# Gated mixer: one activation instruction per two PSUM banks, and the two halves of the hidden layer computed ahead of the spatial product

## The chip, the core and the metric

The kernel runs on one core of one Trainium2 chip. The engines of the core run side by side and wait for each other through semaphores: PE (TensorE, matrix products, with PEld for its weight loads), DVE (VectorE), ACT (ScalarE), POOL (GpSimd) and SP, which issues the DMA transfers. PE writes its products to PSUM, eight banks of 512 float32 columns on 128 partitions; DVE and ACT read them from there. The metric is the device time of one execution in microseconds (us).

## What is computed

Two residual blocks over 2048 tokens of width 448, in bfloat16. The first is a layer norm and a local attention with 16 heads, which the change doesn't touch. The second is a gated mixer with a spatial product over all tokens:

```python
def _B_ref(x, w_in, w_sp, b_sp, w_out):
    B, S, D = x.shape                    # 1, 2048, 448
    F = w_in.shape[-1]                   # 1792
    Fh = F // 2                          # 896
    z = _gelu(jnp.einsum('bsd,df->bsf', x, w_in))
    z1 = z[..., :Fh].copy()
    z2 = _layernorm(z[..., Fh:], axis=-1)
    g = jnp.einsum('ts,bsf->btf', w_sp, z2) + b_sp[None, :, None]
    return jnp.einsum('bsf,fd->bsd', z1 * g, w_out)

h  = x + _A_ref(_layernorm(x, axis=-1), A_wqkv, A_wo)
h2 = h + _B_ref(_layernorm(h, axis=-1), B_w_in, B_w_sp, B_b_sp, B_w_out)
```

`_gelu` is the tanh approximation. The halves of the hidden layer are called z1 (the gate) and z2 (normalised and mixed over the tokens).

## The kernel before

Every instruction is issued through `iss(engine, function, reads, writes)`. It records which resources the instruction reads and writes (`Res` objects, one for a bank, a tile or a block), and works out from that the semaphore waits. Each engine runs its own instructions strictly in the order in which the program issues them, so the order of the calls is the schedule.

The attention part ends with the rows of `x_tm` (16 blocks of 128 tokens) holding h. The mixer then goes through these steps:

- **Hidden input.** `ln_norm_block` (L351, DVE) normalises a block, `tm_transpose_block` (L360 on PE, L369 on DVE) transposes it by way of a PSUM bank into `xhT`. Eight blocks are normalised and transposed, then the other eight. The banks come from a counter over all eight banks, `banksB`, from which four draws for the bias `bb` have been made before.
- **z2.** For each of 16 blocks and each of the two halves of 448 columns, `z2_half_mm` (L744) makes four accumulating matmuls into one bank. A `GeluTile` then computes gelu as x times sigmoid of a cubic: ACT copies the bank to `xb` (`copy`, L708); DVE makes the cubic in three instructions (`front`, L712 to L714); ACT applies Sigmoid (`tanh`, L718); DVE multiplies and sums in one instruction (`back`, L723); ACT squares and sums (`sq`, L733). The steps of successive tiles are staggered by one tile. Three buffers `xb`, `wk`, `tb` rotate.
- **Normalisation of z2.** After all 32 halves, DVE turns the sums into mean and variance, a chain of 16 small instructions makes the reciprocal root (`rsqrt_chain`, L232 to L243), and 16 instructions (L787) normalise the blocks in place.
- **z1, spatial product, gate, output.** A tile is one of 7 chunks of 128 hidden columns (`fc`) by one of 4 chunks of 512 tokens (`tc`). For tile j the program issues the z1 matmuls (`z1_tile_mm`, L755, four of them) and their gelu; for tile j-1 the spatial product (`g_tile_mm`, L800, 16 accumulating matmuls, one for each block of z2); for tile j-2 the gate (`u_tile`, L813 and L815, DVE adds the bias and multiplies with z1 in place). After the seventh tile of a token chunk, `wout_block` makes the output product of four token blocks (L823, seven matmuls each), adds the residual on DVE (L827) and stores (L829, by SP).

The weights `wspT_lo`, `wspT_hi` and `w_out` are loaded by DMAs that SP issues early; the change does not move them.

Of the kernel before, what the change touches and what calls it, by code (L numbers as in the profile page):

```python
# [6 lines left out]
D = 448  # L7
# [22 lines left out]
GELU_C = 0.044715  # L30
GELU_K2 = 1.5957691216057308
# [96 lines left out]
def bass_sequential_preLN__sliding_local_dilated__mixer_gmlp__prompt_kernel(  # L128
# [17 lines left out]
    with contextlib.ExitStack() as top:  # L146
# [20 lines left out]
        s3a = sb("s3a", [128, 2, NB], F32)  # L167
        s3b = sb("s3b", [128, 2, NB], F32)
        junk = sb("junk", [128, 512], BF16)
        junk2 = sb("junk2", [128, 512], BF16)  # L170
# [28 lines left out]
        r_junk2 = Res("junk2")  # L199
# [435 lines left out]
        NGW = 3  # L635
        xb = sb("xb", [128, NGW, 512], BF16, es=stackB)
        wk = sb("wk", [128, NGW, 512], BF16, es=stackB)
        tb = sb("tb", [128, NGW, 512], BF16, es=stackB)
        w_out = sb("w_out", [128, FC7, D], BF16, es=stackB)
        ub = sb("ub", [128, 2, 512], BF16, es=stackB)  # L640
# [15 lines left out]
        r_z2ph = [[bres("z2p_%d_%d" % (m, k)) for k in range(2)] for m in range(NB)]  # L656
        r_s3 = []
        r_xb = [bres("xb%d" % i) for i in range(NGW)]
        r_wk = [bres("wk%d" % i) for i in range(NGW)]
        r_tb = [bres("tb%d" % i) for i in range(NGW)]  # L660
        r_wout = bres("w_out")
        r_ub = [bres("ub0"), bres("ub1")]
# [11 lines left out]
        banksB = gbanks_B  # L674
        gctr = [0]
# [9 lines left out]
        class GeluTile:  # L685
            def __init__(self, out_dst_ap, in_ps_ap, n, rdst, rbank, sum_x_ap=None, sum_sq_ap=None):
                s = gctr[0] % NGW
                gctr[0] += 1
                self.s = s
                self.XB = xb[:, s, 0:n]  # L690
                self.WK = wk[:, s, 0:n]
                self.TB = tb[:, s, 0:n]
                self.out_dst_ap = out_dst_ap
                self.in_ps_ap = in_ps_ap
                self.n = n
                self.rdst = rdst
                self.rbank = rbank
                self.sum_x_ap = sum_x_ap
                self.sum_sq_ap = sum_sq_ap
                if sum_x_ap is not None:  # L700
                    self.rsx = Res("sumx")
                    self.rsq = Res("sumsq")
                    r_s3.append(self.rsx)
                    r_s3.append(self.rsq)

            def copy(self):
                s = self.s
                iss("act", lambda e: e.activation(self.XB, self.in_ps_ap, AF.Copy), reads=[self.rbank], writes=[r_xb[s]])  # L708

            def front(self):  # L710
                s = self.s
                iss("dve", lambda e: e.tensor_tensor(self.WK, self.XB, self.XB, ALU.mult), reads=[r_xb[s]], writes=[r_wk[s]])  # L712
                iss("dve", lambda e: e.tensor_scalar(self.WK, self.WK, GELU_C, 1.0, ALU.mult, ALU.add), reads=[r_wk[s]], writes=[r_wk[s]])  # L713
                iss("dve", lambda e: e.tensor_tensor(self.WK, self.WK, self.XB, ALU.mult), reads=[r_wk[s], r_xb[s]], writes=[r_wk[s]])  # L714

            def tanh(self):
                s = self.s
                iss("act", lambda e: e.activation(self.TB, self.WK, AF.Sigmoid, scale=GELU_K2), reads=[r_wk[s]], writes=[r_tb[s]])  # L718

            def back(self):  # L720
                s = self.s
                if self.sum_x_ap is not None:
                    iss("dve", lambda e: e.tensor_tensor_reduce(self.out_dst_ap, self.TB, self.XB, 1.0, 0.0, ALU.mult, ALU.add,  # L723
                                                               self.sum_x_ap),
                        reads=[r_tb[s], r_xb[s]], writes=[self.rdst, self.rsx])
                else:
                    iss("dve", lambda e: e.tensor_tensor(self.out_dst_ap, self.TB, self.XB, ALU.mult),
                        reads=[r_tb[s], r_xb[s]], writes=[self.rdst])

            def sq(self):  # L730
                if self.sum_sq_ap is None:
                    return
                iss("act", lambda e: e.activation(junk2[:, 0:self.n], self.out_dst_ap, AF.Square, accum_out=self.sum_sq_ap),  # L733
                    reads=[self.rdst], writes=[r_junk2, self.rsq])

        def hn_unit(m):
            ln_norm_block(m, mv2, rstd2, r_ln2, m % NTR)
            tm_transpose_block(m, m % NTR, banksB, "dve")

        def z2_half_mm(m, k):  # L740
            bk = banksB.next()
            out_ap = psum[:, bk * 512: bk * 512 + D]
            for c in range(NCH):
                iss("pe", lambda e, c=c: e.matmul(out_ap, xhT[0:DC, c, PAD + 128 * m: PAD + 128 * m + 128],  # L744
                                                 w_in[:, c, FH + D * k: FH + D * (k + 1)],
                                                 start=(c == 0), stop=(c == NCH - 1)),
                    reads=[r_xhT[m], r_win], writes=[r_bank[bk]])
            return GeluTile(z2p[:, m, D * k:D * (k + 1)], out_ap, D, r_z2ph[m][k], r_bank[bk],
                            s3a[:, k, m:m + 1], s3b[:, k, m:m + 1])

        def z1_tile_mm(fc, tc):
            bk = banksB.next()
            out_ap = psum[:, bk * 512: bk * 512 + 512]
            for c in range(NCH):
                iss("pe", lambda e, c=c: e.matmul(out_ap, w_in[:, c, fc * 128:(fc + 1) * 128],  # L755
                                                 xhT[0:DC, c, PAD + 512 * tc: PAD + 512 * (tc + 1)],
                                                 start=(c == 0), stop=(c == NCH - 1)),
                    reads=[r_win] + r_xhT[4 * tc:4 * tc + 4], writes=[r_bank[bk]])
            return GeluTile(z1p[:, fc, 512 * tc:512 * (tc + 1)], out_ap, 512, r_z1p[fc][tc], r_bank[bk])

        for half in range(2):
            for m in range(8 * half, 8 * half + 8):
                ln_norm_block(m, mv2, rstd2, r_ln2, m % NTR)
            for m in range(8 * half, 8 * half + 8):
                tm_transpose_block(m, m % NTR, banksB, "dve")
        NH = 2 * NB
        live = {}
        for j in range(NH + 3):
            if j < NH:
                m, k = j // 2, j % 2  # L770
                g = z2_half_mm(m, k)
                live[j] = g
                g.copy()
                g.front()
            if 0 <= j - 1 < NH:
                live[j - 1].tanh()
                live[j - 1].back()
            if 0 <= j - 2 < NH:
                live[j - 2].sq()
                del live[j - 2]  # L780

        iss("dve", lambda e: e.tensor_tensor(s3a[:, 0, :], s3a[:, 0, :], s3a[:, 1, :], ALU.add), reads=[r_ln3] + r_s3, writes=[r_ln3])
        iss("dve", lambda e: e.tensor_tensor(s3b[:, 0, :], s3b[:, 0, :], s3b[:, 1, :], ALU.add), reads=[r_ln3], writes=[r_ln3])
        mean_var_from_sums(s3a[:, 0, :], s3b[:, 0, :], float(FH), mv3, r_ln3)
        rstd3 = rsqrt_chain(lambda: mv3[:, 0:NB, 1], 0, NB, EPS, 3, r_ln3)
        for m in range(NB):
            iss("dve", lambda e, m=m: e.tensor_scalar(z2p[:, m, :], z2p[:, m, :], mv3[:, m, 0:1], rstd3[:, m:m + 1],  # L787
                                                     ALU.subtract, ALU.mult),
                reads=[r_z2ph[m][0], r_z2ph[m][1], r_ln3], writes=[r_z2ph[m][0], r_z2ph[m][1]])
# [3 lines left out]
        def g_tile_mm(fc, tc):  # L793
            bk = banksB.next()
            out_ap = psum[:, bk * 512: bk * 512 + 512]
            wsrc = wspT_lo if tc < 2 else wspT_hi
            coff = 512 * (tc % 2)
            hhi = 0 if tc < 2 else 1
            for sbk in range(NB):
                iss("pe", lambda e, sbk=sbk: e.matmul(out_ap, z2p[:, sbk, fc * 128:(fc + 1) * 128],  # L800
                                                     wsrc[:, sbk, coff:coff + 512],
                                                     start=(sbk == 0), stop=(sbk == NB - 1)),
                    reads=[r_z2ph[sbk][0], r_z2ph[sbk][1], r_wspT[2 * sbk + hhi]], writes=[r_bank[bk]])
            gbank[(fc, tc)] = (bk, out_ap)
# [3 lines left out]
        def u_tile(fc, tc):  # L808
            bk, out_ap = gbank[(fc, tc)]
            utile = z1p[:, fc, 512 * tc:512 * (tc + 1)]  # L810
            s = uct[0] % 2
# [6 lines left out]
        def wout_block(m):  # L818
            tc = m // 4
            bk = banksB.next()  # L820
# [73 lines left out]
```

## Time and profile before

| | |
|---|---|
| median of 3 runs | 344.4 us (339.64 to 347.36) |
| span of the profiled execution | 342.4 us |
| mean granted clock of PE in it | 0.915 |
| end of the attention, start of the mixer's hidden input | about 127 us |
| first z2 matmul | 135.6 us |
| first matmul of the spatial product | 196.1 us |
| last residual addition begins | 339.7 us |

The profile is of one execution of its own. Its span runs from the first to the last instruction; the device times of the three runs stand beside it, and no separate device time is given for the profiled one. A row of the timeline is: start in us, duration in us, engine, line, operation, output<-input, shapes, count, and in brackets the idle time ahead of it and the engine that ended it. A row of a group is: line, engine, operation, names, shapes, count, then total busy us and mean ns of one, then the idle time before. A row of the stretches is: from:to, length, busy time and count of instructions (x) of PE, PEld, DVE, ACT and POOL, the granted clock of PE as a share of full speed, the DMA share and GB/s. A row of the chain is start, duration and what ran.

### The profile page before, as it was taken

The page shows a single profiled execution, that of the slowest core. Times are in us where ns is not written, and L with a number is a line of the kernel's source. Part 1 is how long each engine was busy: PE and PEld are TensorE (multiplying, and loading weights), DVE is VectorE, ACT ScalarE, POOL GpSimd, SP SyncE. Part 2 cuts the span into 40 slices and gives each one's busy share as a digit, 9 for nine tenths or more (in the row PEclk, how much of TensorE's full clock was granted, in tenths as well). Part 3 has the DMA queues.
Part 4 walks back from the last instruction along what each step waited for, and adds up shares of the span by engine and source line. Part 5 has one row for each costly group of instructions (what it writes and reads, how often), then busy time and mean ns, then how long its engine had stood idle before and what let it go on. Part 6 is the DMA issues. An engine that isn't in the chain of part 4 may idle for free.

```text
span 342.4 us, 4998 instructions
## 1 busy us (share of the span) xinstructions
PE 287.6 (84%) x1859; PEld 144.9 (42%) x1872; DVE 242.8 (71%) x670; ACT 156.8 (46%) x320; POOL 5.1 (1%) x17
## 2 busy tenths in 40 slices
PE   3789899999998848966550099999999999999996
PEld 1434455555565617521110034444444444444442
DVE  4987446897779779899999896554555565545554
ACT  1435878777866020899999322221222022212220
POOL 5000000000000000000000000000000000000000
PEclk9879989999987556999996589999999999999999
DMA  7999900000000069930000000001000100000001
GB/s 223 258 220 179 190 16 2 2 0 2 3 2 1 2 162 187 161 76 0 0 1 1 0 2 0 0 2 50 3 3 0 38 17 0 0 26 30 1 0 54
DMA packets 40537, 16.39 MB, mean 48 GB/s; under 512 B 34177, under 2 KB 39617, under 8 KB 40514
## 3 DMA queue, kind: packets, MB, share of 16 engines
q1 hardware_dynamic: 40514, 16.08, 22.5%
q8 instruction: 14, 0.23, 0.3%
q14 instruction: 9, 0.07, 0.1%
HBM read 5.85 MB, written 1.84 MB: 22 GB/s over the span
## 4 chain that ended last, share of the span: by engine, by line
PE 66%; DVE 28%; ACT 2%; issue 2%; DMA 1%; ACTq 0%; DVEq 0%
PE psum L800 29%; PE psum L383 9%; PE psum L755 7%; PE psum L823 6%; DVE z2p L723 5%; PE psum L400 4%; PE psum L485 4%; PE psum L444 4%; DVE wk L714 3%; DVE wk L712 3%; DVE wk L713 3%; DVE xhT L369 2%; DVE tring L351 2%; PE psum L416 2%; DVE st L347 1%
## 5 line engine op out<-in xcount | busy, mean ns | idle before, releaser
L708 ACT ACTIVATE xb<-psum 128x448 bf16<-128x448 f32 (+1 forms) x60 | 33.4, 558 | 108.3 <-PE psum L755 95.5
L800 PE MATMUL psum<-wspT_lo,z2p 128*128 128x512 bf16 x217 | 52.7, 388 | 17.9 <-DVE z2p L787 17.4
L712 DVE TENSOR_TENSOR wk<-xb 128x448 bf16<-128x448 bf16 (+1 forms) x60 | 24.2, 404 | 40.1 <-ACT xb L708 40.1
L800 PE MATMUL psum<-wspT_hi,z2p 128*128 128x512 bf16 x218 | 49.7, 379 | 0.3
L423 ACT ACTIVATE E<-psum 128x456 bf16<-128x456 f32 (+1 forms) x72 | 39.6, 550 | 15.1 <-PE psum L472 8.8
L800 PEld LDWEIGHTS psum<-wspT_lo,z2p 128*128 128x128 bf16 x224 | 21.9, 98 | 46.9 <-DVE z2p L787 22.3
L718 ACT ACTIVATE tb<-wk 128x448 bf16<-128x448 bf16 (+1 forms) x60 | 35.9, 598 | 12.7 <-DVE wk L714 12.7
L744 PE MATMUL psum<-w_in,xhT 112*128 112x448 bf16 x128 | 28.7, 365 | 11.1 <-ACT xb L708 11.1
L800 PEld LDWEIGHTS psum<-wspT_hi,z2p 128*128 128x128 bf16 x224 | 21.9, 98 | 26.5
L755 PE MATMUL psum<-xhT,w_in 112*128 112x512 bf16 x112 | 28.8, 379 | 1.2 <-ACT xb L708 1.2
L714 DVE TENSOR_TENSOR wk<-wk,xb 128x448 bf16<-128x448 bf16 (+1 forms) x60 | 24.5, 408 | 2.1
L744 PEld LDWEIGHTS psum<-w_in,xhT 112*128 112x128 bf16 x128 | 11.4, 101 | 28.0 <-ACT xb L708 19.0
L444 PEld LDWEIGHTS psum<-V,E 128*114 128x114 bf16 (+1 forms) x288 | 21.4, 149 | 2.4 <-issue 0.4
L823 PE MATMUL psum<-w_out,z1p 128*128 128x448 bf16 x112 | 22.0, 353 | 0.1
L444 PE MATMUL psum<-V,E 128*114 128x29 bf16 (+1 forms) x288 | 21.7, 210 | 0.0
L485 PE MATMUL psum<-wo,OT 112*128 112x448 bf16 x64 | 18.4, 420 | 3.9 <-DVE OT L475 2.8
L432 DVE TENSOR_TENSOR E<-E,maskb 128x1824 bf16<-128x1824 bf16 (+1 forms) x18 | 19.9, 1103 | 1.8 <-ACT E L423 1.7
L813 DVE TENSOR_TENSOR ub<-psum,bb 128x512 bf16<-128x512 f32 x28 | 19.1, 683 | 2.3 <-PE psum L800 2.3
L723 DVE CUSTOM_DVE_ANT_0 z2p<-tb,xb 128x448 bf16<-128x448 bf16 x32 | 19.8, 618 | 0.9 <-ACT tb L718 0.8
L383 PE MATMUL psum<-xhT,wqp 112*128 112x512 bf16 x64 | 18.1, 440 | 2.3 <-DVE xhT L369 2.3
L827 DVE TENSOR_TENSOR tring<-psum,x_tm 128x448 bf16<-128x448 f32 x16 | 10.0, 624 | 13.5 <-PE psum L823 13.5
L713 DVE TENSOR_SCALAR wk<-wk 128x448 bf16<-128x448 bf16 (+1 forms) x60 | 17.1, 285 | 2.1
(82 smaller groups left out, 338.1 us busy)
## 6 DMA issues: line engine op xcount, KB each, us to landing
x_tm<-in_A_x_dram SPq DMA_DIRECT2D x4, 448.0 KB, 7.2
out_dram<-tring SPq DMA_DIRECT2D x16, 112.0 KB, 1.7
w_in<-in_B_w_in_dram SPq DMA_DIRECT2D x1, 1568.0 KB, 15.5
stg<-in_A_wqkv_dram SPq DMA_DIRECT2D x1, 1176.0 KB, 9.9
w_out<-in_B_w_out_dram SPq DMA_DIRECT2D x1, 784.0 KB, 4.5
wo<-in_A_wo_dram SPq DMA_DIRECT2D x1, 392.0 KB, 12.9
wspT_lo<-in_B_w_sp_dram SPq DMA_TRANSPOSE x16, 4.0
wspT_hi<-in_B_w_sp_dram SPq DMA_TRANSPOSE x16, 4.1
```

The lines of the kernel that those rows point to most:

```text
L383: e.matmul(out_ap, wsrc[:, c, gg, :], xhT[0:DC, c, col0:col0 + 512], start=(c == 0), stop=(c == NCH - 1)),
L423: iss("act", lambda e, in_ap=in_ap, out_e=out_e: e.activation(out_e, in_ap, AF.Exp, scale=SCALE), reads=[r_bank[hh]], writes=[r_E[slot]])
L444: e.matmul(psum[0:nq, ob + h * 32: ob + h * 32 + DH + 1], E[0:nk, slot, eidx, 0:nq], V1[0:nk, vslot, h, 0:DH + 1]),
L708: iss("act", lambda e: e.activation(self.XB, self.in_ps_ap, AF.Copy), reads=[self.rbank], writes=[r_xb[s]])
L712: iss("dve", lambda e: e.tensor_tensor(self.WK, self.XB, self.XB, ALU.mult), reads=[r_xb[s]], writes=[r_wk[s]])
L714: iss("dve", lambda e: e.tensor_tensor(self.WK, self.WK, self.XB, ALU.mult), reads=[r_wk[s], r_xb[s]], writes=[r_wk[s]])
L718: iss("act", lambda e: e.activation(self.TB, self.WK, AF.Sigmoid, scale=GELU_K2), reads=[r_wk[s]], writes=[r_tb[s]])
L723: iss("dve", lambda e: e.tensor_tensor_reduce(self.out_dst_ap, self.TB, self.XB, 1.0, 0.0, ALU.mult, ALU.add, self.sum_x_ap), reads=[r_tb[ ...
L744: iss("pe", lambda e, c=c: e.matmul(out_ap, xhT[0:DC, c, PAD + 128 * m: PAD + 128 * m + 128], w_in[:, c, FH + D * k: FH + D * (k + 1)], st ...
L755: iss("pe", lambda e, c=c: e.matmul(out_ap, w_in[:, c, fc * 128:(fc + 1) * 128], xhT[0:DC, c, PAD + 512 * tc: PAD + 512 * (tc + 1)], start ...
L800: iss("pe", lambda e, sbk=sbk: e.matmul(out_ap, z2p[:, sbk, fc * 128:(fc + 1) * 128], wsrc[:, sbk, coff:coff + 512], start=(sbk == 0), sto ...
L823: iss("pe", lambda e, fc=fc: e.matmul(out_ap, z1p[:, fc, 128 * m:128 * m + 128], w_out[:, fc, :], start=(fc == 0), stop=(fc == FC7 - 1)), ...
```

## The change

Gelu becomes one ACT instruction (`Gelu_apprx_tanh`) that reads two neighbouring PSUM banks and writes the result; the class `GeluTile` with its buffers goes. Banks for z2 and z1 are drawn in pairs from a counter of their own, `PairBanks`, which goes round four pairs. The sums for the layer norm of z2 are made by DVE (`bn_stats` on each half of a block, `bn_aggr` on both), and z2 is normalised after every four blocks instead of after all 16. All z2 blocks come first, then all z1 pairs (128 hidden columns by 1024 tokens), then the spatial product with the gate. The output product of a token chunk is issued after the first product tile of the next chunk; for the last chunk, six of seven matmuls of each of the four blocks come ahead, then the seventh of each with the residual and the store. The bias buffer `ub` has three slots instead of two.

```diff
+        banksB = Banks([0, 1, 2, 3, 4, 5, 6, 7])
+        class PairBanks:
+            def next(self):
+                p = self.i % 4
+                self.i += 1
+                return 2 * p
...
+        def z2_block(m):
+            bk = pairs.next()
+            for k in range(2):
+                out_ap = psum[:, (bk + k) * 512: (bk + k) * 512 + D]
+                for c in range(NCH):
+                    iss("pe", ... e.matmul(out_ap, xhT[0:DC, c, PAD + 128 * m: PAD + 128 * m + 128],
+                                 w_in[:, c, FH + D * k: FH + D * (k + 1)], ...),
+                        reads=[r_xhT[m], r_win], writes=[r_bank[bk + k]])
+            src = psum[:, bk * 512: (bk + 2) * 512].rearrange("p (k n) -> p k n", k=2)[:, :, 0:D]
+            dst = z2p[:, m, :].rearrange("p (k n) -> p k n", k=2)
+            iss("act", lambda e: e.activation(dst, src, AF.Gelu_apprx_tanh),
+                reads=[r_bank[bk], r_bank[bk + 1]], writes=[r_z2p[m]])
+            for k in range(2):
+                iss("dve", lambda e, k=k: e.bn_stats(st3[:, m, k, :], z2p[:, m, D * k:D * (k + 1)]),
+                    reads=[r_z2p[m], r_st3[m]], writes=[r_st3[m]])
+            iss("dve", lambda e: e.bn_aggr(mv3[:, m, :], st3[:, m, :, :]), reads=[r_st3[m]], writes=[r_mv3[m]])
+
+        def z2_finish(lo, hi):
...
+            rstd3 = rsqrt_chain(lambda: mv3[:, lo:hi, 1], lo, hi, EPS, 3, r_ln3)
+            for m in range(lo, hi):
+                iss("dve", lambda e, m=m: e.tensor_scalar(z2p[:, m, :], z2p[:, m, :], mv3[:, m, 0:1],
+                                                         rstd3[:, m - lo:m - lo + 1],
+                                                         ALU.subtract, ALU.mult),
+                    reads=[r_z2p[m], r_ln3], writes=[r_z2p[m]])
+
+        def z1_pair(fc, th):
+            bk = pairs.next()
+            for t in range(2):
+                tc = 2 * th + t
+                out_ap = psum[:, (bk + t) * 512: (bk + t) * 512 + 512]
...
+            src = psum[:, bk * 512: (bk + 2) * 512]
+            dst = z1p[:, fc, 1024 * th:1024 * (th + 1)]
+            iss("act", lambda e: e.activation(dst, src, AF.Gelu_apprx_tanh),
+                reads=[r_bank[bk], r_bank[bk + 1]], writes=[r_z1p[fc][2 * th], r_z1p[fc][2 * th + 1]])
...
+        for m in range(NB):
+            z2_block(m)
+            if m % 4 == 3:
+                z2_finish(m - 3, m + 1)
+        for th in range(2):
+            for fc in range(FC7):
+                z1_pair(fc, th)
         tiles = [(fc, tc) for tc in range(4) for fc in range(FC7)]
+        for j, (fc, tc) in enumerate(tiles):
+            g_tile_mm(fc, tc)
+            u_tile(fc, tc)
+            if fc == 0 and tc > 0:
+                for mm in range(4 * tc - 4, 4 * tc):
+                    bk = banksB.next()
+                    wout_mm(mm, bk, range(FC7))
+                    wout_store(mm, bk)
+        last = []
+        for mm in range(12, 16):
+            bk = banksB.next()
+            last.append(bk)
+            wout_mm(mm, bk, range(FC7 - 1))
+        for mm, bk in zip(range(12, 16), last):
+            wout_mm(mm, bk, [FC7 - 1])
+            wout_store(mm, bk)
```

`wout_mm` is the matmul part of the former `wout_block`, for the chunks it is given; `wout_store` is its residual addition and store.

More of the change, by code (lines that the diff above doesn't have):

```diff
@@ L29 @@
 SCALE = DH ** (-0.5)
-GELU_C = 0.044715
-GELU_K2 = 1.5957691216057308
 RSQ_MAGIC = 0x5F3759DF
@@ L655, in bass_sequential_preLN__sliding_local_dilated__mixer_gmlp__prompt_kernel @@
         r_z2p = [bres("z2p_%d" % m) for m in range(NB)]
[L656 to L660, printed above, removed]
+        r_st3 = [bres("st3_%d" % m) for m in range(NB)]
+        r_mv3 = [Res("mv3_%d" % m) for m in range(NB)]
         r_wout = bres("w_out")
-        r_ub = [bres("ub0"), bres("ub1")]
+        r_ub = [bres("ub%d" % i) for i in range(NU)]
         for sbk in range(NB):
@@ L683, in bass_sequential_preLN__sliding_local_dilated__mixer_gmlp__prompt_kernel @@
                 reads=[r_bank[bk]], writes=[r_bb])
[L685 to L734, printed above, removed]
@@ L736, in hn_unit, with hidden_block @@
-        def hn_unit(m):
+        def hidden_block(m):
             ln_norm_block(m, mv2, rstd2, r_ln2, m % NTR)
             tm_transpose_block(m, m % NTR, banksB, "dve")
[L740 to L789, printed above, removed]
+        def z2_block(m):
[3 more added lines that the diff above has]
+                for c in range(NCH):
+                    iss("pe", lambda e, c=c, k=k, out_ap=out_ap:
+                        e.matmul(out_ap, xhT[0:DC, c, PAD + 128 * m: PAD + 128 * m + 128],
+                                 w_in[:, c, FH + D * k: FH + D * (k + 1)],
+                                 start=(c == 0), stop=(c == NCH - 1)),
+                        reads=[r_xhT[m], r_win], writes=[r_bank[bk + k]])
[7 more added lines that the diff above has]
+            iss("dve", lambda e: e.bn_aggr(mv3[:, m, :], st3[:, m, :, :]), reads=[r_st3[m]], writes=[r_mv3[m]])
@@ new lines, in z1_pair @@
+        def z1_pair(fc, th):
[3 more added lines that the diff above has]
+                out_ap = psum[:, (bk + t) * 512: (bk + t) * 512 + 512]
+                for c in range(NCH):
+                    iss("pe", lambda e, c=c, tc=tc, out_ap=out_ap:
+                        e.matmul(out_ap, w_in[:, c, fc * 128:(fc + 1) * 128],
+                                 xhT[0:DC, c, PAD + 512 * tc: PAD + 512 * (tc + 1)],
+                                 start=(c == 0), stop=(c == NCH - 1)),
+                        reads=[r_win] + r_xhT[4 * tc:4 * tc + 4], writes=[r_bank[bk + t]])
+            src = psum[:, bk * 512: (bk + 2) * 512]
+            dst = z1p[:, fc, 1024 * th:1024 * (th + 1)]
+            iss("act", lambda e: e.activation(dst, src, AF.Gelu_apprx_tanh),
+                reads=[r_bank[bk], r_bank[bk + 1]], writes=[r_z1p[fc][2 * th], r_z1p[fc][2 * th + 1]])
@@ L802, in g_tile_mm @@
                                                      start=(sbk == 0), stop=(sbk == NB - 1)),
-                    reads=[r_z2ph[sbk][0], r_z2ph[sbk][1], r_wspT[2 * sbk + hhi]], writes=[r_bank[bk]])
+                    reads=[r_z2p[sbk], r_wspT[2 * sbk + hhi]], writes=[r_bank[bk]])
             gbank[(fc, tc)] = (bk, out_ap)
@@ L816, in u_tile, with wout_mm @@
                 reads=[r_ub[s], r_z1p[fc][tc]], writes=[r_z1p[fc][tc]])
-        def wout_block(m):
+        def wout_mm(m, bk, fcs):
             tc = m // 4
-            bk = banksB.next()
             out_ap = psum[:, bk * 512: bk * 512 + D]
-            for fc in range(FC7):
+            for fc in fcs:
                 iss("pe", lambda e, fc=fc: e.matmul(out_ap, z1p[:, fc, 128 * m:128 * m + 128], w_out[:, fc, :],
@@ L825, in wout_block, with wout_store @@
                     reads=[r_z1p[fc][tc], r_wout], writes=[r_bank[bk]])
+        def wout_store(m, bk):
+            out_ap = psum[:, bk * 512: bk * 512 + D]
             slot = m % NTR
@@ L829, in wout_block @@
             dma(lambda e: e.dma_start(OUT[128 * m:128 * m + 128, :], tring[:, slot, :]), reads=[r_tr[slot]], store=True)
-        tiles = [(fc, tc) for tc in range(4) for fc in range(FC7)]
-        NT = len(tiles)
-        glive = {}
-        for j in range(NT + 3):
-            if j < NT:
-                fc, tc = tiles[j]
-                gt = z1_tile_mm(fc, tc)
-                glive[j] = gt
-                gt.copy()
-                gt.front()
-            if 0 <= j - 1 < NT:
-                glive[j - 1].tanh()
-                glive[j - 1].back()
-                g_tile_mm(*tiles[j - 1])
-            if 0 <= j - 2 < NT:
-                u_tile(*tiles[j - 2])
-                fc2, tc2 = tiles[j - 2]
-                del glive[j - 2]
-                if fc2 == FC7 - 1:
-                    for jj in range(4):
-                        wout_block(4 * tc2 + jj)
+        for half in range(2):
+            for m in range(8 * half, 8 * half + 8):
+                ln_norm_block(m, mv2, rstd2, r_ln2, m % NTR)
+            for m in range(8 * half, 8 * half + 8):
+                tm_transpose_block(m, m % NTR, banksB, "dve")
+        for m in range(NB):
[5 more added lines that the diff above has]
+                z1_pair(fc, th)
+        tiles = [(fc, tc) for tc in range(4) for fc in range(FC7)]
+        for j, (fc, tc) in enumerate(tiles):
[14 more added lines that the diff above has]
+            wout_store(mm, bk)
         sch.wait_keys("sp", sch.store_keys)
```

25 lines of the change are left out of this document (12 added, 13 removed).

## The prediction

> **What bounds the kernel now.** I read the page first (busy shares and the forty slices), then the busy time by stretch, then one period of the timeline, then the chain that ended last.
>
> ```profile
> span 342.4 us, 4998 instructions
> PE 287.6 (84%) x1859; PEld 144.9 (42%) x1872; DVE 242.8 (71%) x670; ACT 156.8 (46%) x320; POOL 5.1 (1%) x17
> ...
> PE   3789899999998848966550099999999999999996
> ...
> DVE  4987446897779779899999896554555565545554
> ACT  1435878777866020899999322221222022212220
> ...
> PEclk9879989999987556999996589999999999999999
> ```
>
> One slice is 8.56 us. Up to slice 15 runs the attention, which the change leaves alone. In slices 16 to 21 DVE and ACT are full and PE is half idle; in 22 PE does almost nothing and its clock falls. From slice 24 on PE is full and the other two are not. The stretches give the amounts:
>
> ```profile
> 127.30:135.60 8.30, 6.36 (x65) 6.13 (x66) 8.29 (x27) 0.00 (x0) 0.00 (x0) 0.71 1.02 191
> 135.60:147.20 11.60, 11.60 (x58) 5.74 (x56) 10.08 (x33) 9.22 (x21) 0.00 (x0) 0.90 1.20 171
> 147.20:190.50 43.30, 19.15 (x82) 6.18 (x80) 40.76 (x135) 42.84 (x110) 0.00 (x0) 0.91 0.03 7
> 190.50:202.40 11.90, 6.13 (x16) 1.72 (x18) 10.96 (x39) 1.05 (x3) 0.00 (x0) 0.62 0.00 0
> 237.90:268.20 30.30, 30.14 (x140) 13.67 (x141) 18.16 (x43) 7.81 (x14) 0.00 (x0) 1.00 0.03 8
> ```
>
> Columns after the length: PE, PEld, DVE, ACT, POOL busy, granted clock, DMA share, GB/s. From 147.2 to 190.5 ACT is busy 99% and DVE 94% while PE works 19 us of 43. The timeline shows the period:
>
> ```profile
> 169.70 0.93 PE L744 MATMUL psum<-w_in,xhT 112*128 112x448 bf16 x4 [0.65 <-ACT xb L708]
> ...
> 170.02 0.39 DVE L712 TENSOR_TENSOR wk<-xb 128x448 bf16<-128x448 bf16 x1
> ...
> 171.29 0.93 PE L744 MATMUL psum<-w_in,xhT 112*128 112x448 bf16 x4 [0.65 <-ACT xb L708]
> ...
> 171.60 0.39 DVE L712 TENSOR_TENSOR wk<-xb 128x448 bf16<-128x448 bf16 x1
> ```
>
> Each z2 half costs 1.58 us (171.60 - 170.02) and PE waits for a free bank. The later part is the opposite, as pieces of the chain show:
>
> ```profile
> 202.38 0.87 PE psum L755 x4
> 203.25 3.46 PE psum L800 x16
> 206.70 0.86 PE psum L755 x4
> ...
> 232.62 5.30 PE psum L823 x28
> 237.92 0.86 PE psum L755 x4
> ...
> 268.16 5.30 PE psum L823 x28
> ```
>
> From 237.92 to 268.16 seven tiles take 30.24 us, 4.32 each = 0.86 + 3.46, without a seam: PE alone decides, at clock 1.00. So only the stretch from 135.6 to about 202 can give time back; the PE work behind it is the same in both kernels and is only put in another order.
>
> **The change, part by part, in PE's order.**
>
> *Start of z2.* The counter that hands z2 its bank pairs is new and starts at banks 0 and 1. Those were last filled by transposes of blocks 12 and 13 (20 draws, four of them for the bias, so the last four blocks lie in banks 0 to 3). Before, the first z2 half drew bank 4, free after block 8.
>
> ```profile
> 134.86 2.73 DVE L369 COPY xhT<-psum 112x512 bf16<-112x512 bf16 x8
> ...
> 135.58 12.88 PE L744 MATMUL psum<-w_in,xhT 112*128 112x448 bf16 x60
> ...
> 137.82 9.27 PEld L744 LDWEIGHTS psum<-w_in,xhT 112*128 112x128 bf16 x49 [0.22 <-issue]
> 135.79 2.68 PE psum L744 x8
> ```
>
> The eight copies end about 0.34 us apart, the one of block 12 near 136.6. So PE starts z2 at about 136.7, 1.1 us later than now. That is a new wait and a loss.
>
> *z2 on PE.* 128 matmuls as before. The first eight took 2.68 us (slow clock), the 49 weight loads paced by matmuls 9.27/49 = 0.189 each. So 2.68 + 120 x 0.189 = 25.4 us, to 162.1, provided banks come free.
>
> The row bearing on the clock is 0.71 before 135.6 and 0.90 after it. The Trainium skill, "TensorE: Matmul & The Clock Gate", Part 1, says that the array runs at half rate until one free-running window of about 3.4 us has been busy; by that the pause before 136.7 could cost another window, an estimate of 1.7 us, and the sum would be 310.4 us of span in place of 308.7.
>
> *The activation.* Per z2 block this removes two Copies, two Sigmoids, two Squares with accumulator reads on ACT and ten DVE instructions, and adds one ACT instruction of 128x896; per z1 pair it adds one of 128x1024. Neither size nor this function is in the trace; the nearest rows:
>
> ```profile
> L718 ACT ACTIVATE tb<-wk 128x448 bf16<-128x448 bf16 x32 | 18.5, 577 | 0.4 <-DVE wk L714 0.4
> L708 ACT ACTIVATE xb<-psum 128x448 bf16<-128x448 f32 x32 | 16.8, 526 | 12.8 <-PE psum L744 12.8
> L708 ACT ACTIVATE xb<-psum 128x512 bf16<-128x512 f32 x28 | 16.6, 595 | 95.5 <-PE psum L755 95.5
> ...
> 139.06 1.28 ACT L718 ACT_TABLE_LOAD   x1
> ```
>
> Lower bound for 896: one 448-wide instruction, 0.53 us; upper: two Sigmoids, 1.15 us. The rows grow by 69 ns for 64 columns, so 0.53 + 448 x 1.08 ns = 1.01; I take 0.95, and 1.1 for 1024. PE needs 8 x 0.189 = 1.51 us per block and 8 x 0.216 = 1.73 per pair, so ACT is hidden even at the upper bound, with four bank pairs in flight. The one table load stays one (1.28 us, before the first use); it delays the first block's readers only.
>
> Copy, Sigmoid and Square cost 526 to 577 ns for 448 columns here. The Trainium skill, "ScalarE: Activation LUTs", says in its pipeline section that throughput is one element per cycle per lane whatever the function, and gives 186 ns + 0.833 ns per element; for 896 that is an estimate of 0.93 us. The trace agrees for the functions it holds; Gelu is not among them, which is why a rival below keeps it open.
>
> *z1 alone.* 28 groups of four, 0.864 each: 24.2 us, 162.1 to 186.3.
>
> *Statistics and normalisation on DVE.* What ACT's accumulator and the summing product did is now two bn_stats, one bn_aggr per block, and per four blocks one rsqrt chain and four normalisations:
>
> ```profile
> 8.62 0.63 DVE L347 BATCH_NORM_STATS2 st<-x_tm 128x6 f32<-128x448 bf16 x1
> 9.28 0.18 DVE L348 BATCH_NORM_AGGREGATE mv<-st 128x2 f32<-128x6 f32 x1
> 9.50 0.63 DVE L347 BATCH_NORM_STATS2 st<-x_tm 128x6 f32<-128x448 bf16 x1
> ...
> 11.25 0.17 DVE L232 TENSOR_SCALAR rsa<-mv 128x8 f32<-128x8 f32 x1
> ...
> 14.49 2.54 DVE L351 TENSOR_SCALAR tring<-x_tm,mv,rst 128x448 bf16<-128x448 bf16 x8
> 195.08 6.86 DVE L787 TENSOR_SCALAR z2p<-z2p,mv,rst 128x896 bf16<-128x896 bf16 x16
> ```
>
> Start to start: bn_stats 0.66, aggregate 0.22, so 1.54 per block; the chain 14.49 - 11.25 = 3.24; a normalisation 6.86/16 = 0.43. A group of four costs 4 x 1.54 + 3.24 + 4 x 0.43 = 11.1 us. The first block reaches DVE at about 141.6 (PE done 139.4, table load 1.28, ACT 0.95), so four groups end at 141.6 + 44.5 = 186.1. DVE is therefore busy without pause under z2 and z1, and hidden by a hair: the spatial product starts at 186.3 with blocks normalised long ago and needs block 15 only 15 x 0.216 = 3.2 us later, at 189.5. The cover is 3.4 us; whatever DVE takes beyond that is PE idle time. The serial tail of now (190.5 to 196.1, and the first product paced by normalisation) goes.
>
> *Spatial product and output.* 28 x 3.46 = 96.8 and three output groups at 5.30 = 15.9: to 299.0. Their DVE work (0.68 + 0.42 per tile) hides under 3.46, and banks alternate over eight.
>
> *End.* Before:
>
> ```profile
> 333.88 5.74 PE L823 MATMUL psum<-w_out,z1p 128*128 128x448 bf16 x28
> 334.08 0.69 DVE L813 TENSOR_TENSOR ub<-psum,bb 128x512 bf16<-128x512 f32 x1 [2.27 <-PE psum L800]
> 334.81 0.42 DVE L815 TENSOR_TENSOR z1p<-ub,z1p 128x512 bf16<-128x512 bf16 x1
> ...
> 339.67 0.62 DVE L827 TENSOR_TENSOR tring<-psum,x_tm 128x448 bf16<-128x448 f32 x1 [0.70 <-PE psum L823]
> ```
>
> From 333.9 to the end are 8.5 us. Now 24 output matmuls (4.5 us) come before the last gate, which covers the 1.4 us of the last tile on DVE, but the four residual additions then fall together: 24 x 0.189 + 0.189 + about 0.25 to reach DVE, 3 x 0.66 + 0.62, and 342.4 - 340.3 = 2.1 for the store: 9.7 us. The new end costs 1.2 us more. Stores keep their queue and order; nothing else is moved on SP or POOL.
>
> **The sum.** 136.7 + 25.4 + 24.2 + 96.8 + 15.9 + 9.7 = 308.7 us of span, 33.7 under 342.4. Median of the runs shown is 344.4 (339.64 to 347.36), 2.0 over the span; the forecast is 344.4 - 33.7 = 310.7 us.
>
> **The rivals.**
>
> *DVE takes the place as the bound before the product.* For: 44.5 us of dependent small instructions, cover 3.4 us, so it decides from 8% more, about 0.03 us on each of the 128 instructions. Against: every duration is a row of this trace. With 25% more, PE waits 11.1 - 3.4 = 7.7 us: 318 us.
>
> *One instruction over two banks, or this function, costs twice the estimate.* It decides above 1.51 us. For: neither is in the trace. Against: all functions there cost alike. At 2.0 and 2.2 us the sum gains 16 x 0.49 + 14 x 0.47 = 14.4: 325 us.
>
> *Not faster: the granted clock falls under the longer dense run.* PE work from z2 on is 25.4 + 24.2 + 96.8 + 21.2 = 167.6 us; the gain of 33.7 is gone when it is stretched by 1.20, a clock of 0.83 throughout; at 0.80 the time is 353 us. For: clocks of 0.62 and 0.71 stand in this trace. Against: those are the sparse stretches; the dense one has 1.00.
>
> **How the numbers follow.** My forecast 0.72, DVE 0.13, ACT 0.10, clock 0.03, and 0.02 for something that ends near no change. Own range of the forecast: the runs scatter by -4.8 and +3.0, the clock and start by about 1.5: 304 to 316. The range given reaches to DVE's case and part of ACT's: 303 to 322. What can be told from no change is about 2%; only the last two cases are not faster than that: faster 0.95, same 0.02, slower 0.03.
>
> **What would show it.** Right: PE full from 137 on with clock 1.00 after the first microseconds; z2 about 25 us, z1 about 24; ACT instructions near 0.95 and 1.1 us and waiting for PE; DVE full until about 186, then a third busy; product starting at 186 without idle PE; about 9.7 us after the last product. Wrong: PE waiting for z2p at the product's start (DVE), PE waiting for ACT in z2 or z1 (ACT), a clock under 0.9 after 140, or gaps between product tiles.

## The result, and the profile after

The changed kernel took 309.56 us (median of 4 runs, 307.33 to 313.91) against 344.93 us (339.64 to 347.36): ratio 0.901, 95% interval 0.8875 to 0.914. The forecast was 310.7 us, within 303 to 322. Ratios here leave out executions more than 1.5% above the fastest of the same kernel, so they are not quotients of the medians.

The profiled execution is the longest of the four (313.91 us, span 312.2 us), and the excess lies in the attention, which is the same in both kernels: its mixer begins at 132.5 us instead of 127.3. So stages are counted below from the mixer's first normalisation, the row that opens it in each trace. From there the mixer took 342.4 - 127.31 = 215.1 us before and 312.2 - 132.54 = 179.7 us after.

First the page of the changed kernel (busy time, slices, two groups), then a row of its timeline for the mixer's start:

```profile
span 312.2 us, 4629 instructions
PE 289.0 (93%) x1872; PEld 150.7 (48%) x1872; DVE 184.3 (59%) x489; ACT 103.9 (33%) x166; POOL 5.1 (2%) x17
PE   2979979989999998479999999999999999999995
DVE  4896554788774787697999991223433332243332
ACT  1425787866786350403665653000000000000000
PEclk9979998999995555559999999999999999999999
L700 ACT ACTIVATE z2p<-psum 128x896 bf16<-128x896 f32 x16 | 14.7, 917 | 20.8 <-PE psum L694 20.8
L732 ACT ACTIVATE z1p<-psum 128x1024 bf16<-128x1024 f32 x14 | 14.3, 1024 | 9.9 <-PE psum L726 9.9
```

```profile
132.54 2.54 DVE L345 TENSOR_SCALAR tring<-x_tm,mv,rst 128x448 bf16<-128x448 bf16 x8
```

One slice is 7.8 us here. Counted from 0, PE is full from slice 18 to the end; DVE is full in slices 19 to 23 and then a third busy. ACT now waits for PE (20.8 and 9.9 us), where PE waited for ACT. The chain that ended last shows that nothing but PE is left on it:

```profile
141.90 24.39 PE psum L694 x128
166.28 24.17 PE psum L726 x112
190.46 27.63 PE psum L744 x128
218.09 5.30 PE psum L766 x28
223.38 24.17 PE psum L744 x112
247.56 5.30 PE psum L766 x28
252.85 24.17 PE psum L744 x112
277.03 5.30 PE psum L766 x28
282.32 20.72 PE psum L744 x96
303.04 5.31 PE psum L766 x28
```

Each start is the sum of the row above it: z2, z1, product and output run from 141.9 to 308.3 without a seam. And DVE's last normalisations, from the timeline, end 2.7 us before the product begins:

```profile
185.82 1.78 DVE L714 TENSOR_SCALAR z2p<-z2p,mv,rst 128x896 bf16<-128x896 bf16 x4
...
190.29 4.91 PE L744 MATMUL psum<-wspT_lo,z2p 128*128 128x512 bf16 x22
```

### The profile page after: what moved, and what is told of

The parts are those of the page before. It is cut to its first block, busy times and chain, and to the rows that moved or that the text cites. A ratio compares the mean times of both kernels' runs of the same rounds, so it can differ in the third digit from the quotient of the medians.

```text
span 312.2 us, 4629 instructions
## 1 busy us (share of the span) xinstructions
PE 289.0 (93%) x1872; PEld 150.7 (48%) x1872; DVE 184.3 (59%) x489; ACT 103.9 (33%) x166; POOL 5.1 (2%) x17
## 4 chain that ended last, share of the span: by engine, by line
PE 83%; DVE 13%; ACT 1%; DMA 1%; issue 1%; DVEq 0%; ACTq 0%
PE psum L744 31%; PE psum L377 10%; PE psum L694 8%; PE psum L726 8%; PE psum L766 7%; PE psum L479 5%; PE psum L438 5%; PE psum L394 5%; DVE xhT L363 2%; DVE tring L345 2%; PE psum L410 2%; PE psum L466 2%; DVE st L341 2%; ACT E L417 1%; DMA x_tm<-in_A_x_dram 1%
## 5 line engine op out<-in xcount | busy, mean ns | idle before, releaser
L744 PE MATMUL psum<-wspT_lo,z2p 128*128 128x512 bf16 x224 | 48.7, 379 | 0.0
L694 PE MATMUL psum<-w_in,xhT 112*128 112x448 bf16 x128 | 24.4, 353 | 0.3 <-DVE xhT L363 0.3
L726 PE MATMUL psum<-xhT,w_in 112*128 112x512 bf16 x112 | 24.3, 379 | 0.0
L700 ACT ACTIVATE z2p<-psum 128x896 bf16<-128x896 f32 x16 | 14.7, 917 | 20.8 <-PE psum L694 20.8
L703 DVE BATCH_NORM_STATS2 st<-z2p 128x6 f32<-128x448 bf16 x32 | 19.6, 611 | 2.3 <-ACT z2p L700 1.7
L394 PE MATMUL psum<-stg,xhT 112*128 112x448 bf16 (+1 forms) x72 | 18.7, 389 | 0.0
L732 ACT ACTIVATE z1p<-psum 128x1024 bf16<-128x1024 f32 x14 | 14.3, 1024 | 9.9 <-PE psum L726 9.9
L354 PE MATMUL psum<-ident,tring 128*112 128x128 bf16 x128 | 12.3, 268 | 5.6 <-DVE tring L345 5.6
L726 PEld LDWEIGHTS psum<-xhT,w_in 112*128 112x128 bf16 x112 | 10.9, 98 | 13.2
L766 PEld LDWEIGHTS psum<-w_out,z1p 128*128 128x128 bf16 x112 | 11.0, 98 | 10.4
```

The source lines that it names most:

```text
L394: iss("pe", lambda e, c=c: e.matmul(out_ap, xhT[0:DC, c, t0:t0 + nk], stg[:, c, 2 * D:3 * D], start=(c == 0), stop=(c == NCH - 1)), reads= ...
L703: iss("dve", lambda e, k=k: e.bn_stats(st3[:, m, k, :], z2p[:, m, D * k:D * (k + 1)]), reads=[r_z2p[m], r_st3[m]], writes=[r_st3[m]])
L726: e.matmul(out_ap, w_in[:, c, fc * 128:(fc + 1) * 128], xhT[0:DC, c, PAD + 512 * tc: PAD + 512 * (tc + 1)], start=(c == 0), stop=(c == NCH ...
L766: iss("pe", lambda e, fc=fc: e.matmul(out_ap, z1p[:, fc, 128 * m:128 * m + 128], w_out[:, fc, :], start=(fc == 0), stop=(fc == FC7 - 1)), ...
```

## The experiments

Each kernel differs from one of the two by the edit shown. Ratios are to the kernel before, run on the same chip beside it; the mixer is the span less the start of the first normalisation, from one profile each. Their starts and spans:

| kernel | first normalisation, span (us) | mixer (us) | ratio of times, 95% interval |
|---|---|---|---|
| before | 127.31, 342.4 | 215.1 | 1 |
| changed | 132.54, 312.2 | 179.7 | 0.901 (0.888 to 0.914) |
| changed, second time | 126.79, 306.4 | 179.6 | 0.900 (0.894 to 0.905) |
| activation alone | 125.10, 309.8 | 184.7 | 0.917 (0.914 to 0.921) |
| order alone | 125.00, 347.8 | 222.8 | 1.032 (1.023 to 1.040) |
| one instruction per bank | 124.12, 303.7 | 179.6 | 0.894 (0.888 to 0.900) |
| z1 beside its tile | 124.98, 331.8 | 206.8 | 0.974 (0.965 to 0.983) |
| gelu twice | 133.89, 316.9 | 183.0 | 0.907 (0.901 to 0.913) |
| one more chain per group | 123.97, 310.8 | 186.8 | 0.920 (0.912 to 0.928) |
| Copy for gelu | 125.08, 304.7 | 179.6 | one execution, 306.6 us |
| other start and end | 124.39, 303.4 | 179.0 | 0.891 (0.886 to 0.896) |
| the same, PE busy before | 127.06, 304.7 | 177.6 | 0.891 (0.885 to 0.897) |

The changed kernel was run a second time, beside some of the others:

> The changed kernel as it is, for comparison with the other kernels of this set: 309.6 us (306 to 313). Nothing is told apart by it alone.

It gave 308.21 us, and the same mixer to 0.1 us though the attention took 5.8 us less.

**The activation alone**, in the order of before:

```diff
             def copy(self):
-                iss("act", lambda e: e.activation(self.XB, self.in_ps_ap, AF.Copy), reads=[self.rbank], writes=[r_xb[s]])
+                iss("act", lambda e: e.activation(self.out_dst_ap, self.in_ps_ap, AF.Gelu_apprx_tanh),
+                    reads=[self.rbank], writes=[self.rdst])
+            def stats(self, m, k):
+                iss("dve", lambda e: e.bn_stats(st3[:, m, k, :], self.out_dst_ap),
+                    reads=[self.rdst, r_st3[m]], writes=[r_st3[m]])
+                if k == 1:
+                    iss("dve", lambda e: e.bn_aggr(mv3[:, m, :], st3[:, m, :, :]), reads=[r_st3[m]], writes=[r_ln3])
...
-                g.front()
...
+                g.stats(m, k)
```

> The kernel before with the new activation alone: gelu in one ACT instruction per bank, bn_stats and bn_aggr on DVE, everything else (order, one chain and 16 normalisations after all of z2, single banks) as it was. My theory: the activation brings most of the gain, because z2 turns from 1.58 us per half into PE's 0.76; what stays is the serial tail, chain 3.3 us and normalisations 6.9 us, during which PE has only two z1 tiles to do: about 7 us of idle PE. Time about 316 us (312 to 320). Rival, the order is what counts and ACT alone little: 335 us or more. Rival, the order brings nothing: 309 to 311 us.

It took 312.08 us. The mixer fell by 30.4 us of the 35.4. What the order still adds is seen in the timeline of this kernel at the end of z2:

```profile
162.38 6.86 DVE L755 TENSOR_SCALAR z2p<-z2p,mv,rst 128x896 bf16<-128x896 bf16 x16
...
163.37 6.31 PE L768 MATMUL psum<-wspT_lo,z2p 128*128 128x512 bf16 x15 [4.13 <-DVE z2p L755]
```

PE idles 4.1 us and then runs the first product at DVE's pace, 6.3 us instead of 3.5: 7.0 us, as expected. Only 5.0 remain in the sum (184.7 against 179.7), because this kernel begins z2 8.0 us after the first normalisation instead of 9.4 (its first bank is free earlier), and ends 8.6 instead of 9.3 us after its last output product begins, all by the timelines.

**The order alone**, with the old five-step gelu:

```diff
-        for j in range(NT + 3):
+        for j in range(NT + 1):
             if j < NT:
                 fc, tc = tiles[j]
                 gt = z1_tile_mm(fc, tc)
                 glive[j] = gt
                 gt.copy()
                 gt.front()
             if 0 <= j - 1 < NT:
                 glive[j - 1].tanh()
                 glive[j - 1].back()
-                g_tile_mm(*tiles[j - 1])
...
+        for j in range(NT):
+            fc, tc = tiles[j]
+            g_tile_mm(fc, tc)
+            u_tile(fc, tc)
+            if fc == 0 and tc > 0:
+                for mm in range(4 * tc - 4, 4 * tc):
+                    wout_block(mm)
+        for mm in range(12, 16):
+            wout_block(mm)
```

> The kernel before with the new order alone: all z1 tiles with the old five-step gelu ahead of the spatial product, then the product, gate and output. My theory: slower than before, because z1 alone is then bound by DVE, 1.47 us per tile by 28 tiles = 41 us where PE needs 24 us that were hidden under the product before: about +17 us, 362 us (355 to 370). Rival, the order itself is worth the serial tail: 337 us.

Slower than before, as the theory said, but by 7.7 us of mixer instead of 17. Its timeline at the end of z1:

```profile
225.09 1.04 PE L755 MATMUL psum<-xhT,w_in 112*128 112x512 bf16 x4 [0.42 <-ACT xb L708]
...
226.85 18.51 PE L800 MATMUL psum<-wspT_lo,z2p 128*128 128x512 bf16 x84 [0.73 <-ACT xb L708]
...
232.88 0.42 DVE L712 TENSOR_TENSOR wk<-xb 128x512 bf16<-128x512 bf16 x1
234.01 0.42 DVE L727 TENSOR_TENSOR z1p<-tb,xb 128x512 bf16<-128x512 bf16 x1
```

z1 does go at DVE's pace, but PE begins the product at 226.9 while DVE still makes gelu tiles: PE's matmuls for z1 run ahead of DVE by the banks that are filled and waiting. DVE's gelu of z1 runs from 198.2 to 239.6, the 41 us that I had priced, but the last 12.7 of them lie under the product, and the price left that overlap out. It leaves 41 - 24 - 12.7 = 4.3 us; the rest, up to 7.7, I did not trace. The order alone thus costs 7.7 us with the old activation. With the new one the rest of the change gives 5.0 us: the order, the normalisation after every four blocks, and another start and end.

**One instruction per bank** instead of one per two:

```diff
-            iss("act", lambda e: e.activation(dst, src, AF.Gelu_apprx_tanh),
-                reads=[r_bank[bk], r_bank[bk + 1]], writes=[r_z2p[m]])
+            for k in range(2):
+                iss("act", lambda e, k=k: e.activation(dst[:, k], src[:, k], AF.Gelu_apprx_tanh),
+                    reads=[r_bank[bk + k]], writes=[r_z2h[m][k]])
```

(and likewise for the two banks of a z1 pair)

> The changed kernel with one gelu instruction per bank (128x448 and 128x512) instead of one per two banks. My theory: ACT needs about 2 x 0.5 us per z2 block against 1.51 us of PE, so it stays hidden and the two-bank form is worth nothing: within 1 us of the changed kernel. Rival, the number of ACT instructions matters: 30 more at about 0.1 us of fixed cost, 312 to 315 us.

The mixer is the same, 179.6 us; the 1.3 us by which its median lies below the changed kernel's (306.87 against 308.21) lies outside the mixer by these two profiles, in the attention's scatter. The groups show why the form doesn't matter:

```profile
L702 ACT ACTIVATE z2p<-psum 128x448 bf16<-128x448 f32 x32 | 17.4, 543 | 17.8 <-PE psum L695 17.8
L735 ACT ACTIVATE z1p<-psum 128x512 bf16<-128x512 f32 x28 | 16.7, 597 | 7.5 <-PE psum L728 7.5
```

ACT works 34.1 us instead of 29.0, and still waits for PE.

**Copy in place of gelu**, as the price of the function:

```diff
-            iss("act", lambda e: e.activation(dst, src, AF.Gelu_apprx_tanh),
+            iss("act", lambda e: e.activation(dst, src, AF.Copy),
```

> The changed kernel with a plain Copy in place of gelu in z2 and z1 (so gelu is left out). My theory: duration depends on the number of columns, not on the function: 128x896 at 0.92 us and 128x1024 at 1.02 us as with gelu, time unchanged within the scatter, 305 to 314 us. Rival, gelu costs more per element than a copy: the Copies come out under 0.85 and 0.95 us.

```profile
L700 ACT ACTIVATE z2p<-psum 128x896 bf16<-128x896 f32 x16 | 14.7, 917 | 22.1 <-PE psum L694 22.1
L732 ACT ACTIVATE z1p<-psum 128x1024 bf16<-128x1024 f32 x14 | 14.3, 1025 | 9.9 <-PE psum L726 9.9
```

917 and 1025 ns, with gelu 917 and 1024: the function costs nothing beside a copy. The 128 columns between them cost 108 ns, 0.84 ns each. The Trainium skill, "ScalarE: Activation LUTs", "Step-by-step: what each stage is for", has 0.833 ns per element for all 19 functions tried; the trace agrees.

**Each gelu twice**, to see how much room ACT has:

```diff
+            for _ in range(2):
                 iss("act", lambda e: e.activation(dst, src, AF.Gelu_apprx_tanh),
```

> The changed kernel with each gelu instruction issued twice (same source and destination). Theory: ACT then needs about 1.85 to 1.95 us per z2 block and 2.05 to 2.15 per z1 pair, above PE's 1.52 and 1.73, and the mixer grows by 8 to 11 us, counted from its first normalisation (179.6 us in the changed kernel): 188 to 191. Rival: four bank pairs in flight and the later product absorb it, 180 us.

The mixer grew by 3.3 us, not 8 to 11. In its chain ACT has become the link:

```profile
145.91 1.73 ACT z2p L701 x2
147.67 1.73 ACT z2p L701 x2
...
174.13 1.95 ACT z1p L734 x2
176.10 1.95 ACT z1p L734 x2
...
195.00 27.79 PE psum L746 x128
```

Two instructions come every 1.76 us (147.67 - 145.91) in z2 and 1.97 in z1, against PE's 1.52 and 1.73. That is 0.24 us over for 30 pairs of banks, 7.2 us; but PE runs ahead into the free pairs, and ACT's z1 group, which ends at 200.8 by the row below, does its last 5.8 us under the first product. So the banks and the later product absorb more than half of it, which is the rival's part.

```profile
173.08 27.68 ACT L734 ACTIVATE z1p<-psum 128x1024 bf16<-128x1024 f32 x28
```

I had priced the doubled instruction at 1.85 to 1.95 and 2.05 to 2.15: two in a row take less than twice one (1.76 against 2 x 0.92, 1.97 against 2 x 1.02). Even at 1.76 and 1.97 the price, which lets nothing overlap, would be 7.2 and not 3.3, so the overlap is the larger part of the miss.

**One more chain per group**, DVE work without a use:

```diff
+            rsqrt_chain(lambda: mv1[:, lo:hi, 1], lo, hi, EPS, 0, r_ln1)
             rstd3 = rsqrt_chain(lambda: mv3[:, lo:hi, 1], lo, hi, EPS, 3, r_ln3)
```

> The changed kernel with one more rsqrt chain (16 small DVE instructions, 3.2 us, result unused) in each of the four groups: 12.9 us more on DVE. By the trace of the changed kernel DVE ends 187.6 us and the last block is needed at 193.7, a cover of 6.1 us, so PE should idle about 6.8 us: 316 us. By the cover as predicted, 3.4 us: 9.5 us idle, 319 us. If DVE were no limit at all here: 310 us.

It took 316.22 us, and the mixer grew by 7.2 us. In its timeline PE waits for z2 before the last four matmuls of the first product:

```profile
188.82 1.78 DVE L715 TENSOR_SCALAR z2p<-z2p,mv,rst 128x896 bf16<-128x896 bf16 x4
189.39 0.10 PEld L745 LDWEIGHTS psum<-wspT_lo,z2p 128*128 128x128 bf16 x1 [5.41 <-DVE z2p L715]
189.39 10.89 PE L745 MATMUL psum<-wspT_lo,z2p 128*128 128x512 bf16 x39 [4.91 <-DVE z2p L715]
```

The last four normalisations begin 64.85 us after the first normalisation (188.82 - 123.97), in the changed kernel 53.28 (185.82 - 132.54): DVE is 11.6 us later, and PE idles 4.9. So 6.7 us were hidden: that is the cover, counted at block 12, the first of the last four (by the changed kernel's trace 6.1 us at block 15). The other 2.3 us stand behind the wait: the 39 matmuls from 189.39 take 10.9 us where 39 x 0.216 are 8.4, and the granted clock is 0.50 from 189.39 to 193. The forecast from the cover of 6.1 us (6.8 us idle) came close to the loss, but counted all of it as idle time.

**z1 beside its tile** instead of ahead of the product:

```diff
-        for th in range(2):
-            for fc in range(FC7):
-                z1_pair(fc, th)
...
+            if tc % 2 == 0:
+                z1_pair(fc, tc // 2)
             g_tile_mm(fc, tc)
```

> The changed kernel with each z1 pair issued just before its product tile instead of all of z1 ahead. My theory: z1 is the cover for the 43 us that DVE needs for statistics and normalisation; without it PE reaches the first product about 22 us earlier and waits for the last normalised blocks, about 17 us idle and then a slow clock for a few: 326 us (323 to 330). Rival, the order does not matter because PE's work is the same: 310 us.

It took 336.8 us, a ratio of 0.982 (0.974 to 0.990); the profiled execution took 571 us, with the matmuls of the product recorded at 0.68 us each where the changed kernel has 0.38, though the granted clock stands at 1.00, and shows nothing of the order. What slowed it is not known. A second run:

> The changed kernel with each z1 pair issued just before its product tile, a second time, for a profile that shows where the time goes. Expected now: 333 to 338 us as timed, 24 us over the changed kernel. Theory: DVE ends its statistics and normalisation about 55 us after the mixer's first normalisation, PE reaches the first product 22 us before that, so some 18 us are idle in front of the last blocks of the first product and the rest is a slow clock afterwards. Rival: the pairs and product tiles fight for banks in every tile, and the loss is spread over the whole product.

337.22 us. The mixer is 27.2 us longer than the changed kernel's. PE in its timeline:

```profile
160.28 1.89 PE L744 MATMUL psum<-wspT_lo,z2p 128*128 128x512 bf16 x8
168.16 1.89 PE L744 MATMUL psum<-wspT_lo,z2p 128*128 128x512 bf16 x4 [5.98 <-DVE z2p L714]
178.80 1.89 PE L744 MATMUL psum<-wspT_lo,z2p 128*128 128x512 bf16 x4 [8.76 <-DVE z2p L714]
180.48 3.62 PE L726 MATMUL psum<-xhT,w_in 112*128 112x512 bf16 x8
...
193.68 1.90 PE L726 MATMUL psum<-xhT,w_in 112*128 112x512 bf16 x8 [0.79 <-DVE ub L757]
196.69 3.63 PE L744 MATMUL psum<-wspT_lo,z2p 128*128 128x512 bf16 x16 [1.12 <-ACT z1p L732]
```

The first product takes until 180.7 instead of 163.7, 17 us, of which 14.7 are two waits for normalised blocks: the theory's part. The first pair behind it takes 3.6 us instead of 1.9; the granted clock is 0.61 from 181 to 185. Most of the remaining 8.5 is the rival's: tiles and pairs draw banks from two counters and meet, and from 180.6 on PE waits for a bank seven times, 0.8 to 1.2 us each, 7.3 in sum. Both were right, and I had priced only the first in the first forecast (326 us).

**Another start and end.** Bank pairs begin at banks 4 and 5; in the last chunk the finish of each block follows six matmuls of the next:

```diff
-                self.i = 0
+                self.i = 2
...
-        for mm, bk in zip(range(12, 16), last):
-            wout_mm(mm, bk, [FC7 - 1])
-            wout_store(mm, bk)
+        last = [banksB.next() for _ in range(4)]
+        wout_mm(12, last[0], range(FC7 - 1))
+        for i in range(4):
+            if i < 3:
+                wout_mm(13 + i, last[i + 1], range(FC7 - 1))
+            wout_mm(12 + i, last[i], [FC7 - 1])
+            wout_store(12 + i, last[i])
```

> The changed kernel with two small edits: the bank pairs start at banks 4 and 5, which are free earlier, and in the last chunk the seventh matmul of each block follows six of the next block, so that the four residual additions are spread. My theory: PE starts z2 about 0.3 to 1.1 us earlier, counted from the first normalisation, and from the last product to the end are 8.1 us in place of 9.2: about 1.5 us off the span, 308 us. Rival, the starting wait is not the bank but PE's own transposes at the slow clock: start unchanged, 1 us from the end alone.

The mixer fell by 0.6 us, not 1.5. By the chain PE began z2 8.6 us after the first normalisation (133.00 - 124.39) instead of 9.4, but z2 took longer:

```profile
129.94 3.06 PE psum L354 x32
133.00 25.18 PE psum L694 x128
158.18 24.17 PE psum L726 x112
```

25.2 against 24.4: z1 ends 58.0 us after the first normalisation, 57.9 in the changed kernel. No bank holds z2 now; it starts right behind PE's own transposes, which take 3.06 us here and 2.57 in the kernel with the activation alone. So the rival holds in part: the bank was worth 0.8 us, and then the transposes bind. The 0.6 us come from the end (by the chain 8.5 instead of 9.2 us after the last output product begins).

**The same with PE busy before z2**, by unused matmuls in its two pauses:

```diff
+        def keep_busy(n, bk):
+            for _ in range(n):
+                iss("pe", lambda e: e.matmul(bank_cols(bk, 512), ident[:, :], warm[:, :]),
+                    reads=[r_ident, r_warm], writes=[r_bank[bk]])
         for half in range(2):
+            keep_busy((12, 4)[half], 4)
```

> The kernel with the earlier start and the spread end, and in addition 12 unused matmuls on PE in the pause before the first eight transposes and 4 in the pause between the eights. Theory: in the kernel with the earlier start PE began z2 1.0 us sooner and lost 0.8 of it to a slower clock in the first matmuls; with PE busy before, z2 runs at full clock from its start and the mixer takes 178.1 to 178.4 us (179.0 without them). Rival, the slow first matmuls have another cause (weights or data still arriving): 179.0 us, first matmuls slow as before.

The mixer took 177.6 us, 2.0 less than the changed kernel's and 1.4 less than without the unused matmuls. First, without them, the stretch ahead of z2 and the first 3 us of z2; then, with them, the last transposes and the first 0.8 us of z2 (rows of the stretches of the two kernels):

```profile
124.40:133.00 8.60, 6.55 (x65) 6.27 (x66) 8.60 (x28) 0.00 (x0) 0.00 (x0) 0.70 1.07 193
133.00:136.00 3.00, 3.00 (x12) 1.34 (x11) 1.68 (x6) 0.49 (x1) 0.00 (x0) 0.70 0.99 191
```

```profile
132.50:136.00 3.50, 3.40 (x37) 2.82 (x38) 3.50 (x13) 0.00 (x0) 0.00 (x0) 1.00 1.06 203
```

The granted clock is 0.70 in both rows without them and 1.00 in the row with them. The Trainium skill, "TensorE: Matmul & The Clock Gate", Part 1, says that the clock is full only after a busy window of some 3.4 us, and that the window runs freely; these rows agree with the first. The second leaves something open: the activation-alone kernel began z2 as early without such matmuls and without slow ones, so one profile each doesn't separate the unused matmuls from the window's luck. The two kernels' medians (305.49 and 306.2 us, on two chips) don't separate them either.

## Why the prediction was right

Its steps, from the first normalisation on:

| step | predicted (us) | measured in the changed kernel (us) |
|---|---|---|
| start of z2 | 9.4 | 9.4 |
| z2 on PE | 25.4 | 24.4 |
| z1 on PE | 24.2 | 24.2 |
| ACT, 128x896 and 128x1024 | 0.95, 1.1 | 0.92, 1.02 |
| DVE's end of normalisation | 58.8 | 55.1 |
| cover of DVE | 3.4 (block 15) | 6.1 (block 15), 6.7 (block 12, by the added chains) |
| product and three outputs | 112.7 | 112.6 |
| end after the last product | 9.7 | 9.2 |
| mixer | 181.4 | 179.7 |

The reason holds: only the stretch up to the product could give time back, and it gave 35.4 us. The activation alone, in the old order, gives 30.4 of them, and the rest of the change 5.0 more, mainly because 24 us of PE work lie over DVE's tail. That cover is needed in the changed kernel: without it (z1 beside its tile) 27.2 us are lost, 17 of them in the first product.

Not all of this is the price of the order. The kernel with the activation alone has z1 beside its tile too, and its first product loses 7.0 us, not 17. It makes one chain and 16 normalisations after all blocks, and its DVE is done 44.1 us after the first normalisation (162.38 + 6.86 - 125.10), against 55.0 with z1 beside its tile and 55.1 in the changed kernel, which make a chain for every four blocks. Three more chains at 3.2 us (the last one runs from 182.61 to 185.82 in the changed kernel) and the later start of z2 (1.4) make up that difference. By these numbers one chain with z1 ahead would let DVE end some 9 us sooner and raise the cover to about 15 us, an estimate. So it is z1 that hides DVE's tail, and normalising by fours makes the tail longer. No kernel with one chain and z1 ahead was run.

Where the terms were off:

- *The start.* I counted the later bank as a loss of 1.1 us. The wait is there, and z2 starts when I said, but PE idles only 0.3 us for it: its own transposes end at 141.64, just before. Taking the wait away (other start) moved z1's end by nothing in that profile, because the first matmuls ran at a lower clock; with PE kept busy before, z1 ended 1.3 us sooner (56.6 us after the first normalisation, against 57.9).
- *z2.* I charged eight slow matmuls, 2.68 us. In the changed kernel the 128 matmuls took 24.39 us, 0.19 each, from the first on: when z2 began, the slow period was over (granted clock 1.00 from 141.9 to 144.9). The second slow period that the prediction weighs at 1.7 us did not come either; with the other start 0.8 us were lost that way.
- *DVE.* It ended 3.7 us earlier than worked out. Its first block came 2.3 us earlier: the first matmuls were not slow (1.0), and the table load (1.3), which I put between them and the first gelu, ran long before. Later blocks cost 1.39 us instead of 1.54, as two blocks of this timeline show:

```profile
130.44 1.28 ACT L700 ACT_TABLE_LOAD   x1
...
178.19 0.21 DVE L705 BATCH_NORM_AGGREGATE mv<-st 128x2 f32<-128x12 f32 x1
178.31 1.23 DVE L703 BATCH_NORM_STATS2 st<-z2p 128x6 f32<-128x448 bf16 x2
179.58 0.21 DVE L705 BATCH_NORM_AGGREGATE mv<-st 128x2 f32<-128x12 f32 x1
```

  Start to start of two aggregates is 1.39 (179.58 - 178.19): the next block's statistics begin 0.12 after an aggregate starts, where the old rows, in which the next instruction waited for it, had 0.22.
- *The rivals.* DVE's was the right one to fear, but starts beyond 6 us, not 3.4. ACT's was priced at 14 us for instructions of 2.0 and 2.2 us, and adds every excess up; with two gelus, 1.76 and 1.97 us, that sum gives 7 and the mixer grew by 3.3, because ACT's last work goes under the first product. Of the clock's nothing was seen: the granted clock stands at 1.00 from 150 us on.

That the total came within 1.1 us is luck: the mixer was 1.7 us shorter than forecast, and the attention alone differed by 5.8 us between two profiles of the changed kernel.

## What to carry to other kernels

A saturated pair of engines ahead of a matmul phase is worth what that phase idles, no more: here 30 us for one fused activation, whether it reads one bank or two. An order pays only with the durations it was made for; z1 ahead of the product cost 7.7 us with the old activation and is part of a gain of 5.0 with the new one. Before moving work, ask which serial tail it covers, and measure the cover by adding work of known length until the waiting engine idles.

## What the runs showed that I had not expected

The attention, identical in all kernels, ends anywhere between 124.0 us (one more chain) and 133.9 (gelu twice). The stretch of the two profiles that I compared first differs in the granted clock, 0.66 before and 0.50 in the changed kernel:

```profile
95.00:127.30 32.30, 25.95 (x241) 16.54 (x239) 26.18 (x77) 13.06 (x25) 0.00 (x0) 0.66 0.14 37
```

```profile
95.00:127.30 32.30, 30.82 (x239) 19.92 (x238) 21.79 (x55) 10.97 (x21) 0.00 (x0) 0.50 0.00 1
```

That stage has pauses on PE, and its length varies by up to 10 us. Time and clock go together: the four executions of the changed kernel took 307.33, 308.75, 310.36 and 313.91 us at mean granted clocks of 0.944, 0.938, 0.933 and 0.912. This scatter lies ahead of the mixer, which repeats to 0.1 us counted from its own first instruction (179.7 and 179.6 in the changed kernel, 179.6 with one instruction per bank and with Copy). That the clock makes the difference is likely but not shown; what sets the moment at which it falls was not tried.
